# Four scheduling edits in one linear-attention and gated-MLP kernel: Newton steps for pairs of token tiles, weight statistics a step later, sums after divisions, and another product order at the start

## The chip, the cores and the metric

The kernel runs on one core of one Trainium2 chip. The metric is device time in microseconds (us) of that core, from the first to the last instruction, over several executions; medians are given with their range. Executions in which the chip grants the tensor engine a lower clock are kept apart as slow runs; everything compared here counts as fast (mean granted clock 0.999 or 1.000 in the profiled runs, down to 0.996 in some of the others; what this does to the ratios is said below the table of the experiments).

The engines are named as the profile names them: PE is the tensor engine, DVE is VectorE, ACT is ScalarE, POOL is GpSimd, SP is SyncE.

## The reference

```python
# x: 1 x 2048 x 1024 bf16; wqkv: 1024 x 3072; wo: 1024 x 1024; w_gate, w_up: 1024 x 3584; w_down: 3584 x 1024
def _A_ref(x, wqkv, wo):                       # linear attention, 32 heads of 32
    q, k, v = ...                              # split of x @ wqkv
    phi = lambda t: jnp.where(t > 0, t + 1, jnp.exp(t)) + 1e-6
    pq, pk = phi(q), phi(k)
    kv = jnp.einsum("bhsd,bhse->bhde", pk, v)
    z = jnp.einsum("bhsd->bhd", pk)
    num = jnp.einsum("bhqd,bhde->bhqe", pq, kv)
    den = jnp.einsum("bhqd,bhd->bhq", pq, z)[..., None] + 1e-6
    return (num / den)... @ wo

def _B_ref(x, w_gate, w_up, w_down):
    return (silu(x @ w_gate) * (x @ w_up)) @ w_down

xn = _layernorm(A_x)                           # over the 1024 columns of a token
return A_x + _A_ref(xn, ...) * silu(_B_ref(xn, ...))
```

## The kernel before

The 2048 tokens are 16 tiles of 128. The stages, in order of time in the profile of before, are:

- the **K stage** (to 130 us): for each token tile, LayerNorm, four K/V column products of eight matmuls, and the small products `kvz` (phi(K) transposed times V) of the tile before;
- the **Q stage** and its mixes (130 to 218 us): Q products, numerator and denominator products (**ND**), their division, the output product (**S**);
- the last ND and S work, in which S is computed for two tiles at a time with fewer multiplications (**S units**: sums of inputs on DVE, then products called x, w, y and so on) (218 to 250 us);
- gate/up and down, twice (250 to 759 us).

Beside the K and Q stages the gate/up/down weights of the later stages are prepared: loaded, squared and summed for a power-of-two scale, scaled, and turned into differences on POOL.

The LayerNorm of one token tile starts with statistics on DVE, takes 1/sqrt(variance) by Newton steps on POOL, and ends with the normalise on DVE:

```python
def grp_of(i):
    return i                       # one token tile per group
def grp_tiles(gid):
    return [gid]

NR_ITERS = 3
def emit_rstd(gid, eng=None):
    eng = eng or nc.gpsimd
    mv, rstd, tiles = grp_state[gid]
    n = len(tiles)
    # ... a first guess ("seed") with three small DVE operations; y and a are 128 x n
    for _ in range(NR_ITERS):
        eng.tensor_tensor(out=w[:, 0:n], in0=y, in1=y, op=ALU.mult)
        eng.tensor_tensor(out=w[:, 0:n], in0=w[:, 0:n], in1=a[:, 0:n], op=ALU.mult)
        eng.tensor_scalar(out=w[:, 0:n], in0=w[:, 0:n], scalar1=-0.5, scalar2=1.5, ...)
        eng.tensor_tensor(out=y, in0=y, in1=w[:, 0:n], op=ALU.mult)

def ln_pre(i, eng=None):
    emit_stats(i)                  # DVE bn_stats, bn_aggr
    emit_rstd(grp_of(i), eng)
```

The K loop. `emit_N` is the normalise of a tile, `emit_Bev` of columns 0 and 1 is phi (exp and relu on ACT, two operations on DVE for each column):

```python
PRE_AT = {2: (5, 6), 3: (7, 8), 4: (9, 10), 5: (11, 12), 6: (13, 14), 7: (15,)}
for i in range(2, NT):
    for c in range(NCH):                       # 4 columns
        ...
        emit_Bmm(i, c)                         # 8 matmuls
        if c == 0:
            ...
            emit_C(i - 1)                      # kvz, reads phi(K) of tile i-1
        emit_Bev(i, c)
        if c == 3 and i in (4, 5, 6, 7):
            prep(1)                            # one weight a step further
        if i >= 8 and c % 2 == 1:
            k = 2 * (i - 8) + c // 2
            prep(13 * (k + 1) // 16 - 13 * k // 16)
        if c % 2 == 1:
            for k in (PRE_AT[i - 1] if i - 1 in PRE_AT else ...)[c // 2:c // 2 + 1]:
                emit_N(k)                      # normalise a tile whose statistics came one tile earlier
            for k in PRE_AT.get(i, ())[c // 2:c // 2 + 1]:
                ln_pre(k)                      # statistics and Newton of a later tile
```

A step of weight preparation, and the start of the S units:

```python
def prep_step(between=None):
    # ... load a new weight, store a finished one
    k3 = prep_st.popleft()
    if prep_st[1] is not None:
        emit_st0(*prep_st[1])                  # ACT square of a weight loaded two steps ago
    if k3 is not None:
        emit_st1(k3[0], stat_ps[0]())          # PE sum over partitions
    # ...

u["sums"]()                                    # four DVE sums
nds[0]()                                       # ND product of a tile, DVE divisions
u["x"]()
u["w"]()                                       # w needs the first sum
emit_S(1, 3, 0, fx[4])
nds[1]()                                       # needs the PSUM buffer that the divisions read
units[1]["sums"]()
u["y"]()
u["x2"]()
emit_S(1, 3, 1, fx[4])
```

## Time and profile before

| | before |
|---|---|
| median of 3 runs | 764.59 us (764.06 to 765.7) |
| span of the profiled run, granted clock | 763.0 us, 1.000 |
| PE waits listed | 8.51 us in nine waits |
| after the last matmul | about 4.1 us |

The first part of the page gives busy time, share of the span and instruction count of each engine:

```profile
...
PE 750.1 (98%) x3731; PEld 349.4 (46%) x3731; DVE 561.8 (74%) x1058; ACT 376.2 (49%) x526; POOL 290.0 (38%) x400
...
```

PE is busy 98% of the span, so only about 13 us could be had without taking away matmuls. The list of waits of PE says where they are. Each line is the waiting tile and its line in the kernel, what ended the wait, then total us, number of waits, the longest:

```profile
PE nd L713 <- DVE wq_sb L725: 2.6, 1, 2.6
PE warm_ps L560 <- DVE warm L557: 1.5, 1, 1.5
PE kv_ps L525 <- DMA wkv_sb<-in_A_wqkv_dram: 1.5, 1, 1.5
PE q_ps L182 <- DVE pqT L162: 1.2, 2, 0.9
PE kv_ps L525 <- DVE pk_sb L162: 1.1, 2, 0.9
PE kv_ps L525 <- ACT xnT L514: 0.4, 1, 0.4
PE kv_ps L525 <- ACT r_t L160: 0.3, 1, 0.3
```

The largest wait is `nd`, once, for `wq_sb`, which is the division of the ND product before. The timeline of PE has it at 224.64 us (columns: start us, duration us, engine, line, operation, output and inputs, shapes, count; in brackets the idle time just before and its releaser):

```profile
...
224.64 0.64 PE L713 MATMUL nd<-KVZ,pqT 128*128 128x132 bf16 x8 [2.58 <-DVE wq_sb L725]
...
```

The timeline of DVE at the same place shows what the divisions queued behind:

```profile
...
218.19 0.45 DVE L779 TENSOR_TENSOR wq_sb<-oT 128x512 f16<-128x512 bf16 x1
...
221.27 1.26 DVE L782 TENSOR_TENSOR oT<-oT,wq_sb 128x512 f16<-128x512 bf16 x1
...
223.23 1.35 DVE L725 TENSOR_TENSOR wq_sb<-nd,rden 128x384 bf16<-128x384 f32 x3
...
```

The four sums (L779 to L782, the first and the last shown) fill 218.2 to 222.5 us, and the divisions (L725) start at 223.23 us. VectorE takes its instructions in the order of the program (the Trainium skill, "Perfetto Trace Analysis", Tensor Engine Instruction, calls its queue strict FIFO, and no instruction in these lines passes another).

### The profile page before, as it was taken

What the parts mean: (1) busy time and instruction counts of PE and PEld (TensorE: products, weight loads), DVE (VectorE), ACT (ScalarE), POOL (GpSimd) and SP (SyncE); (2) the same over time, 40 slices, a digit from 0 to 9 for tenths busy, and PEclk for the clock granted to TensorE, in tenths of its full rate; (3) what the DMA queues carried; (4) which work ended last, traced back from release to release, by engine and by line L of the source; (5) the groups of instructions that cost most, each with busy time, mean ns of one, the idle gap of its engine ahead of it and who ended that gap; (6) DMA issues with size and microseconds to landing.
All of it is one profiled execution on the core that took longest, in us unless ns stands there. A gap on an engine that the chain in (4) does not pass through costs nothing.

```text
span 763.0 us, 10573 instructions
## 1 busy us (share of the span) xinstructions
PE 750.1 (98%) x3731; PEld 349.4 (46%) x3731; DVE 561.8 (74%) x1058; ACT 376.2 (49%) x526; POOL 290.0 (38%) x400
## 2 busy tenths in 40 slices
PE   8999999999989999999999999999999999999997
PEld 3444444454444444444444444444444444444444
DVE  6788797687587788888889885358676767787335
ACT  4778866799855656666557411132323222211022
POOL 0477899998540265868686000110000000200000
PEclk9999999999999999999999999999999999999999
DMA  9877899859659669897889227398655445530824
GB/s 318 291 153 144 232 297 305 303 121 304 181 169 272 232 228 307 298 348 288 303 296 371 106 82 264 112 342 324 245 185 184 166 165 169 173 141 15 275 89 133
DMA packets 105845, 170.30 MB, mean 223 GB/s; under 512 B 34688, under 2 KB 82176, under 8 KB 95168
## 3 DMA queue, kind: packets, MB, share of 16 engines
q1 hardware_dynamic: 100144, 144.99, 59.2%
q0 software_dynamic: 4208, 22.15, 7.3%
q10 hardware_dynamic: 1440, 2.49, 1.1%
q8 instruction: 29, 0.48, 0.3%
q14 instruction: 24, 0.20, 0.1%
HBM read 111.67 MB, written 50.59 MB: 213 GB/s over the span
## 4 chain that ended last, share of the span: by engine, by line
PE 70%; DVE 1%; ACT 0%; issue 0%
PE zw L935 25%; PE xb L935 13%; PE dzw L1120 12%; PE yb L935 6%; PE dx L1120 6%; PE dy L1120 3%; PE fx L786 3%; PE df L1120 1%; PE dz L1120 0%; PE fx L744 0%; PE nd L713 0%; DVE wq_sb L725 0%; DVE wq_sb L781 0%; DVE oT L782 0%; DVE wq_sb L780 0%; DVE pqT L150 0%
## 5 line engine op out<-in xcount | busy, mean ns | idle before, releaser
L935 PEld LDWEIGHTS <-w_sb 128*128 128x128 f16 (+1 forms) x1568 | 152.1, 98 | 182.8
L525 PE MATMUL kv_ps<-wkv_sb,xnT 128*128 128x512 bf16 x512 | 114.1, 379 | 3.3 <-DMA wkv_sb<-in_A_wqkv_dram 1.5
L935 PE MATMUL xb<-xnT,w_sb 128*128 128x512 bf16 x448 | 115.0, 379 | 0.0
L935 PE MATMUL zw<-S,w_sb 128*128 128x512 f16 x448 | 105.8, 379 | 0.0
L935 PE MATMUL zw<-xnT,w_sb 128*128 128x512 bf16 x448 | 105.8, 379 | 0.0
L294 POOL TENSOR_TENSOR w_sb<-w_sb 128x512 f16<-128x512 bf16 x42 | 50.3, 1197 | 97.8 <-DVE w_sb L282 53.2
L259 ACT ACTIVATE w_sb<-w_sb 128x2048 bf16<-128x2048 bf16 x42 | 79.9, 1903 | 13.1 <-DMA w_sb<-in_B_w_up_dram 6.5
L1120 PE MATMUL dx<-w_sb,hT 128*128 128x512 bf16 x210 | 79.6, 379 | 0.0
L525 PEld LDWEIGHTS <-xnT 128*128 128x128 bf16 x512 | 48.4, 97 | 59.2 <-issue 3.9
L1120 PEld LDWEIGHTS <-hT 128*128 128x128 bf16 (+1 forms) x462 | 45.2, 98 | 51.7
L182 PE MATMUL q_ps<-xnT,wq_sb 128*128 128x512 bf16 x256 | 58.7, 379 | 1.2 <-DVE pqT L162 1.2
L1120 PE MATMUL dzw<-w_sb,hT 128*128 128x512 f16 x196 | 58.3, 379 | 0.0
L1011 ACT ACTIVATE sg<-cg 128x1024 bf16<-128x1024 f32 x28 | 29.6, 1057 | 57.4 <-DVE cg L1004 57.4
L935 PE MATMUL yb<-S,w_sb 128*128 128x512 f16 x224 | 57.4, 378 | 0.0
L1004 DVE SCALAR_TENSOR_TENSOR cg<-zw,rc_all,s 128x1024 f32<-128x1024 f32 x28 | 35.9, 1283 | 25.2 <-PE zw L935 13.5
L1060 POOL TENSOR_TENSOR hs<-hT 128x512 f16<-128x512 bf16 x2 | 2.5, 1255 | 132.6 <-ACT sg L1011 132.6
L963 DVE SCALAR_TENSOR_TENSOR s<-yb,rc_all,s 128x512 f32<-128x512 f32 x42 | 31.4, 748 | 28.0 <-ACT s L962 28.0
L295 POOL TENSOR_TENSOR w_sb<-w_sb 128x512 f16<-128x512 bf16 x42 | 50.8, 1209 | 3.3
L297 POOL TENSOR_TENSOR w_sb<-w_sb 128x512 f16<-128x512 bf16 x42 | 50.5, 1203 | 0.0
L296 POOL TENSOR_TENSOR w_sb<-w_sb 128x512 f16<-128x512 bf16 x42 | 50.1, 1192 | 0.0
L1094 POOL DMA_DIRECT2D out_dram<-io x16 | 8.7, 542 | 101.9 <-DVE io L1093 101.6
L962 ACT ACTIVATE s<-xb,rcl 128x512 f32<-128x512 f32 x14 | 9.6, 687 | 65.3 <-PE xb L935 65.3
(183 smaller groups left out, 1203.2 us busy)
## 6 DMA issues: line engine op xcount, KB each, us to landing
w_sb<-pk_g SPq DMA_DIRECT2D x27, 1024.0 KB, 6.0
pk_g<-w_sb SPq DMA_DIRECT2D x14, 1024.0 KB, 5.0
w_sb<-wd SPq DMA_DIRECT2D x14, 1024.0 KB, 5.3
w_sb<-pk_u SPq DMA_DIRECT2D x14, 1024.0 KB, 5.0
pk_u<-w_sb POOLq DMA_DIRECT2D x13, 1024.0 KB, 5.2
w_sb<-wd SPq DMA_DIRECT2D x14, 768.0 KB, 5.8
w_sb<-in_B_w_gate_dram SPq DMA_DIRECT2D x14, 512.0 KB, 5.9
w_sb<-in_B_w_down_dram SPq DMA_DIRECT2D x28, 256.0 KB, 4.9
```

The lines of the kernel that those rows point to most:

```text
L182: nc.tensor.matmul(q_ps[:], lhsT=wq_sb[:, dc, g * P:(g + 1) * P], rhs=xn_ap(dc, btok), start=(dc == 0), stop=(dc == DC - 1))
L259: nc.scalar.activation(out=junk, in_=raw_view(key, t), func=ACT.Square, accum_out=asum[:])
L294: nc.gpsimd.tensor_tensor(out=T1, in0=b12, in1=b11, op=ALU.subtract)
L295: nc.gpsimd.tensor_tensor(out=T2, in0=b22, in1=T1, op=ALU.subtract)
L296: nc.gpsimd.tensor_tensor(out=T3, in0=b22, in1=b12, op=ALU.subtract)
L297: nc.gpsimd.tensor_tensor(out=T4, in0=b21, in1=T2, op=ALU.subtract)
L525: mm = nc.tensor.matmul(kv_ps[:], lhsT=xn_ap(dc, tok), rhs=wkv_sb[:, dc, c * CW:(c + 1) * CW], start=(dc == 0), stop=(dc == DC - 1))
L935: mm = nc.tensor.matmul(out, lhsT=lhs(k), rhs=rhs(k), start=(first and k == 0), stop=(k == HK - 1), skip_group_check=True)
L963: nc.vector.scalar_tensor_tensor(out=s2[:], in0=y_[:], scalar=rc, in1=s1[:], op0=ALU.mult, op1=ALU.add)
L1004: nc.vector.scalar_tensor_tensor(out=d12, in0=zw[:], scalar=rc, in1=s2[:, None, :].to_broadcast([P, 2, TB]), op0=ALU.mult, op1=ALU.add)
L1011: nc.scalar.activation(out=sg[:, 1:3, :], in_=cf[:], func=ACT.Silu)
L1120: nc.tensor.matmul(out, lhsT=lhs, rhs=rhs, start=first, stop=lastk, skip_group_check=True)
```

## The change

The change has four parts. (1) The Newton steps of two neighbouring token tiles are done in one chain on 128x2 operands, with half as many POOL instructions. (2) The square of a prepared weight comes one step later, so that its load has had longer to land, and the preparations are spread differently: one more before tile 8, 11 in place of 13 in tiles 8 to 15, two in place of one in Q block 0. (3) The sums of the first S unit are issued behind the divisions. (4) At the start of the K stage the second product is that of tile 1, column 0, in place of tile 0, column 1, whose weights come later.

```diff
@@ weights                                                       (part 2)
+    PREP_AT = ((4, 3), (5, 3), (6, 1), (6, 3), (7, 3))
@@ prep_step
-        if prep_st[1] is not None:
-            emit_st0(*prep_st[1])
+        if prep_st[0] is not None:
+            emit_st0(*prep_st[0])
@@ LayerNorm groups                                              (part 1)
+        GRP = {5: (5, 6), 6: (5, 6), 7: (7, 8), 8: (7, 8), 9: (9, 10), 10: (9, 10), 11: (11, 12), 12: (11, 12),
+               13: (13, 14), 14: (13, 14)}
         def grp_of(i):
-            return i
+            return grp_tiles(i)[0]
         def grp_tiles(gid):
-            return [gid]
+            return GRP.get(gid, (gid,))
@@ ln_pre
             emit_stats(i)
-            emit_rstd(grp_of(i), eng)
+            if i == grp_tiles(i)[-1]:
+                emit_rstd(grp_of(i), eng)
@@ start of the K stage                                          (part 4)
         emit_Bev(0, 0)
+        emit_Bmm(1, 0)
+        emit_N(2)
         emit_Bmm(0, 1)
-        emit_N(2)
-        emit_Bmm(1, 0)
+        emit_Bev(1, 0)
+        ln_pre(3)
         emit_Bev(0, 1)
-        ln_pre(3)
-        emit_Bev(1, 0)
@@ K loop and Q block 0                                          (part 2)
-                if c == 3 and i in (4, 5, 6, 7):
+                if (i, c) in PREP_AT:
                     prep(1)
-                    prep(13 * (k + 1) // 16 - 13 * k // 16)
+                    prep(11 * (k + 1) // 16 - 11 * k // 16)
-            if g == 3:
+            if g in (2, 5):
                 prep(1)
@@ S units                                                       (part 3)
-        u["sums"]()
         nds[0]()
         u["x"]()
-        u["w"]()
+        u["sums"]()
         emit_S(1, 3, 0, fx[4])
         nds[1]()
+        u["w"]()
+        emit_S(1, 3, 1, fx[4])
         units[1]["sums"]()
         u["y"]()
         u["x2"]()
-        emit_S(1, 3, 1, fx[4])
```

## The prediction

> **What bounds it now.** TensorE: the page gives 750.1 us busy of 763.0 at full clock. Of the other 12.9 us, 8.6 are nine waits (1.5 at the start) and about 4.1 follow the last matmul. No PE wait lies after 225 us (gate/up/down). List of waits and PE timeline:
> - 2.58 us at 224.6: the second ND product waits for VectorE's divisions of the first (one PSUM buffer), which sit behind the four S-unit sums (218.2 to 222.5).
> - 1.46 us at 11.1: K product (tile 0, column 1) waits for its weight DMA; 0.33 us at 20.7: a bank waits for a ScalarE eviction.
> - 0.18 and 0.95 us late in the K stage, 0.24 and 0.93 us in Q block 0: banks wait for VectorE phi, and that for ScalarE exp.
>
> **What the change does.**
> 1. *Sums behind divisions.* They (0.36 + 0.35 + 1.35 us) can then run from 218.6 to 220.8, while PE has x and an S product until 221.0. Sums took 0.45, 1.20, 1.37, 1.26 us here, 0.42 later; GpSimd ran until 222.2. That agrees with the Trainium skill, "SBUF — State Buffer", Who interferes with whom: two-input VectorE operations contend with GpSimd reads. w and y should find their sums ready. Gain 2.3 to 2.6 us.
> 2. *Newton pairs.* 13 groups become 8; 60 GpSimd operations of 0.26 us go, and 15 VectorE ones of 0.15 us. None is on PE's chain, but GpSimd's Newton ends at 78.5 us and delays the weight differences, which run without gap from 85.7 to 151.8, about 5 us per tile, while 13 preparations were asked for in 59 us (4.5 us each). Stores and loads queue behind.
> 3. *Statistics one step later, preparations respread* (one earlier; 11, not 13, in tiles 8 to 15; two in Q). Before, ScalarE's squares wait 6.6 us in five waits for weight DMAs (list of waits); ScalarE is strict FIFO (Trainium skill, "Perfetto Trace Analysis", Tensor Engine Instruction), so exp and phi come late. At 11 per 59 us GpSimd keeps pace and loads land a step ahead. Of 2.3 us I expect 1.7 to 2.3 back. In the ND stage squares end 1.7 us before their sum matmuls: no new wait. VectorE in Q block 0 gets fuller (estimate 15.8 us of work against 14.3 of PE); five banks cover that.
> 4. *K order.* Product (tile 1, column 0) fills the DMA wait, but needs ScalarE's transposed copy (10.24 us); VectorE's Newton for tile 2 and phi stay bound by the x DMA at 11.74 us, so the tile 2 transpose and the bank freed at 20.6 us come hardly earlier. The wait moves there; net 0.1 to 0.3 us.
>
> **Sum.** 2.5 + 2.0 + 0.15 = 4.6 us. Predicted **760.0 us**, 80% range **758.4 to 762.8**. Faster by over 2%: 0.01; within 2%: 0.98; slower by over 2%: 0.01.
>
> **What would show it.** Right: PE waits after 100 us fall from 4.9 us to under 0.8; no square waits for a DMA in the K stage; GpSimd starts weight differences near 75 us and has gaps before 150; the ND wait is gone; the first 21 us keep 3 to 3.8 us of PE idle, differently named. Wrong on 4: K tile 2 starts a microsecond earlier.
>
> **What would make it wrong.** New PE waits on a square or on phi in Q block 0; w or y waiting for sums; Newton pairs delaying a transpose; a DMA wait as gate/up begins.

## More of the kernel before

The timeline of DVE in the K stage, cut to the last seed operation of a Newton chain (L469) and to the normalise (L482), shows a tile being normalised and another being seeded alternately:

```profile
...
57.55 0.15 DVE L469 TENSOR_SCALAR rstd<-rstd 128x1 int32<-128x1 int32 x1
58.25 0.55 DVE L482 TENSOR_SCALAR xn<-xp,mv,rstd 128x1024 bf16<-128x1024 bf16 x1 [0.55 <-POOL rstd L477]
...
60.65 0.15 DVE L469 TENSOR_SCALAR rstd<-rstd 128x1 int32<-128x1 int32 x1
...
62.92 0.53 DVE L482 TENSOR_SCALAR xn<-xp,mv,rstd 128x1024 bf16<-128x1024 bf16 x1
...
65.30 0.15 DVE L469 TENSOR_SCALAR rstd<-rstd 128x1 int32<-128x1 int32 x1
66.01 0.55 DVE L482 TENSOR_SCALAR xn<-xp,mv,rstd 128x1024 bf16<-128x1024 bf16 x1 [0.55 <-POOL rstd L477]
...
```

The two short waits for POOL are 0.55 us. The normalise at 58.25 us and the one at 66.01 us are 7.76 us apart, for two token tiles' statistics; PE takes 7.37 us for a tile of the K loop. POOL is busy without a gap here: it has two chains of twelve Newton operations to serve per K tile (the work of the K stage for one token tile). No PE wait lies here, so the small lag was covered.

## The result, and the profile after

| | before | after |
|---|---|---|
| median | 764.33 us (763.88 to 765.7, 4 runs) | 765.62 us (765.03 to 766.42, 4 runs) |
| span of the profiled run, granted clock | 763.0 us, 1.000 | 764.6 us, 0.999 |
| PE waits listed | 8.51 us | 9.21 us |

The ratio of the two is 1.0015, with a 95% interval of 0.9997 to 1.0032. Ratios here and below are worked out from the fast runs of the same rounds, so they are not quite the ratio of the medians. The expected 4.6 us did not show. The first part of the page of after:

```profile
...
PE 751.0 (98%) x3731; PEld 349.3 (46%) x3731; DVE 556.3 (73%) x1043; ACT 376.2 (49%) x526; POOL 277.9 (36%) x340
...
```

POOL has the 60 instructions and 12 us less that the change was to take away. The list of waits of PE of after (lines are four or five higher in this kernel than in before):

```profile
PE kvz L551 <- DVE pk_sb L163: 2.8, 4, 1.3
PE kv_ps L529 <- DVE pk_sb L163: 1.5, 1, 1.5
PE warm_ps L565 <- DVE warm L562: 1.5, 1, 1.5
PE xb L940 <- ACT sg L1015: 1.2, 1, 1.2
PE kvz L551 <- ACT w_sb L260: 0.5, 1, 0.5
PE fx L791 <- DVE wq_sb L784: 0.5, 1, 0.5
PE kv_ps L529 <- ACT xnT L518: 0.5, 1, 0.5
PE kv_ps L529 <- DVE xnT L516: 0.3, 1, 0.3
PE tr_ps L513 <- DVE xn L486: 0.2, 1, 0.2
PE yb L264 <- DVE s L968: 0.2, 1, 0.2
```

The large `nd` wait, the two `q_ps` waits and the DMA wait `kv_ps <- wkv_sb` are gone, as intended. In their place stand `kvz` for `pk_sb`, four times, `kvz` once for `w_sb`, and `kv_ps` for `pk_sb`, 1.53 us: together 4.9 us, all in the K stage, where before had no PE wait between 21 and 112 us. `pk_sb` is phi(K). The timeline of PE of after has them at these times (three of the six):

```profile
...
63.80 0.40 PE L551 MATMUL kvz<-v_sb,pk_sb 128*128 128x129 bf16 x4 [0.55 <-DVE pk_sb L163]
...
74.42 0.40 PE L551 MATMUL kvz<-v_sb,pk_sb 128*128 128x129 bf16 x4 [1.29 <-DVE pk_sb L163]
...
87.94 3.61 PE L529 MATMUL kv_ps<-wkv_sb,xnT 128*128 128x512 bf16 x16 [1.53 <-DVE pk_sb L163]
...
```

They come about 9 us apart in pairs. The timeline of DVE of after shows the loop behind them:

```profile
...
53.53 0.17 DVE L473 TENSOR_SCALAR rstd<-rstd 128x2 int32<-128x2 int32 x1
...
54.13 0.69 DVE L163 SCALAR_TENSOR_TENSOR pk_sb<-e_t,r_t 128x512 bf16<-128x512 f32 x1
...
55.19 0.69 DVE L163 SCALAR_TENSOR_TENSOR pk_sb<-e_t,r_t 128x512 bf16<-128x512 f32 x1
58.18 0.55 DVE L486 TENSOR_SCALAR xn<-xp,mv,rstd 128x1024 bf16<-128x1024 bf16 x1 [2.29 <-POOL rstd L481]
...
60.08 0.49 DVE L486 TENSOR_SCALAR xn<-xp,mv,rstd 128x1024 bf16<-128x1024 bf16 x1
...
62.45 0.17 DVE L473 TENSOR_SCALAR rstd<-rstd 128x2 int32<-128x2 int32 x1
...
```

L473 is the last seed operation; L163 is the second half of phi; L486 is the normalise. DVE seeds a pair at 53.53 us, does two phi (to 55.9 us), then stands for 2.29 us until POOL's chain is done, normalises both tiles and takes the statistics of the next pair, and seeds that at 62.45 us: a period of 8.92 us. The timeline of POOL of after, cut to the first, the second and the last of the twelve operations of that pair's chain:

```profile
...
53.78 0.30 POOL L477 TENSOR_TENSOR lnw<-rstd 128x2 f32<-128x2 f32 x1 [4.56 <-DVE rstd L473]
54.15 0.72 POOL L478 TENSOR_TENSOR lnw<-lnw,lna 128x2 f32<-128x2 f32 x1
...
57.95 0.19 POOL L481 TENSOR_TENSOR rstd<-rstd,lnw 128x2 f32<-128x2 f32 x1
```

The chain runs from 53.78 to 58.14 us, 4.4 us; between chains POOL stands idle for 4.56 us. So the period is a sum of two things that no longer overlap: 4.4 us of POOL from seed to last Newton operation, and 4.5 us of DVE from that to the next seed. A K tile of PE is 7.37 us, so DVE falls behind by 1.5 us a tile, and phi with it. Before, the first tile of each pair had a chain of its own that began half a K tile earlier.

To compare parts of the kernels that a single time can't tell apart, the next table gives milestones read from the timeline of PE of each profiled run: the first `kvz` product of the K loop, the first Q product, the first ND product of the last block, the first gate product, the first product of the down stage of the first pass, and the end of the last matmul. All are us from the start of the span.

| run | first kvz | first Q | last block's ND | gate/up 1 | down 1 | last matmul |
|---|---|---|---|---|---|---|
| before | 25.85 | 130.43 | 217.98 | 250.52 | 420.24 | 758.86 |
| after | 25.05 | 134.30 | 220.04 | 250.50 | 421.92 | 760.54 |

After arrives at the first Q product 3.9 us later than before, makes 1.8 us of it good in Q and the mixes and 2.1 us in the last ND block (30.46 us in place of 32.54), and is level at gate/up. Then it loses 1.7 us in gate/up of pass 1 (171.4 us in place of 169.7), where its list of waits has `xb` for `sg`, 1.2 us. The releaser `sg` is an ACT operation, late because a square before it had waited for a weight's DMA, as the timeline of ACT of after shows:

```profile
...
329.75 1.91 ACT L260 ACTIVATE w_sb<-w_sb 128x2048 bf16<-128x2048 bf16 x1 [5.93 <-DMA w_sb<-in_B_w_up_dram]
...
```

### The profile page after: what moved, and what is told of

It is laid out like the page before. It is cut to its first block, busy times and chain, and to the rows that moved or that the text cites. A ratio compares the mean times of both kernels' runs of the same rounds, so it can differ in the third digit from the quotient of the medians.

```text
span 764.6 us, 10494 instructions
## 1 busy us (share of the span) xinstructions
PE 751.0 (98%) x3731; PEld 349.3 (46%) x3731; DVE 556.3 (73%) x1043; ACT 376.2 (49%) x526; POOL 277.9 (36%) x340
## 4 chain that ended last, share of the span: by engine, by line
PE 84%; DVE 6%; POOL 4%; DMA 3%; issue 2%; ACT 1%; SPq 0%; ACTq 0%; POOLq 0%
PE zw L940 23%; PE dzw L1125 12%; PE xb L940 12%; PE q_ps L183 7%; PE dx L1125 6%; PE yb L940 6%; PE kv_ps L529 6%; PE s_ps L749 3%; PE dy L1125 3%; PE fx L791 3%; DVE stats L448 2%; DMA w_sb<-in_B_w_up_dram 2%; POOL lnw L478 1%; DMA xp<-in_A_x_dram 1%; POOL rstd L481 1%
```

## The experiments

Kernels are compared only within the same rounds. The theory that the runs had to test (here theory P, for pairs) is the loop above: the paired chain is long and DVE stands waiting for it, so phi is late. The rival (theory R) is that the later statistics and the respread preparations made the K-stage waits, because they too move DVE and ACT work into tiles 6 to 9.

| run | median us (range, runs) | before | ratio, 95% interval |
|---|---|---|---|
| e0_after_again | 765.16 (764.91 to 766.53, 6) | 765.79 | 0.9999, 0.9983 to 1.0015 |
| e1_no_pairs | 759.82 (759.0 to 762.14, 6) | 765.79 | 0.993, 0.9912 to 0.9948 |
| e2_pairs_only | 771.24 (770.44 to 773.42, 6) | 765.79 | 1.0078, 1.0059 to 1.0097 |
| e3_stats_first | 759.29 (758.69 to 760.36, 6) | 765.79 | 0.992, 0.9904 to 0.9935 |
| e4_two_iters | 758.85 (758.32 to 759.69, 4) | 765.45 | 0.9919, 0.9902 to 0.9935 |
| e5_nd_only | 762.44 (761.96 to 765.8, 4) | 765.45 | 0.9974, 0.9948 to 1.0 |
| e6_korder_only | 765.29 (764.01 to 767.25, 4) | 765.45 | 1.0004, 0.9982 to 1.0026 |
| e7_stats_prep_only | 762.15 (761.86 to 762.81, 4) | 765.45 | 0.9964, 0.9945 to 0.9982 |
| e10_stats_first_again | 759.39 (758.73 to 760.43, 6) | 766.19 | 0.9914, 0.9891 to 0.9938 |
| e8_z_bank | 758.92 (758.6 to 760.79, 6) | 766.19 | 0.9914, 0.9888 to 0.994 |
| e9_z_bank_io | 760.79 (759.0 to 762.66, 6) | 766.19 | 0.9933, 0.9906 to 0.9959 |

All gave the reference's result. All executions counted as fast, but a part of these ratios goes with the granted clock. In the call of e10 the executions of before took 763.82 to 764.5 us at a mean clock of 0.999 or 1.000 (four of them) and 765.68 to 768.26 us at 0.997 or 0.998 (seven), while all executions of e1, e3, e4 and e7 to e10 had 0.999 or 1.000. With the executions at 0.999 or above alone, the plain means give 1.001 for e0, 0.994 for e1, 0.993 for e3, 0.992 for e4, 0.996 for e5, e7 and e9, 1.000 for e6, and 0.994 for e10 and e8 (no interval was worked out for these; e2 has a single such execution). Whether the kernel has a part in the clock is open. The milestones come from profiles at 0.999 or 1.000 and are free of this. The milestones of the profiled runs:

| run | first kvz | first Q | last block's ND | gate/up 1 | down 1 | last matmul |
|---|---|---|---|---|---|---|
| e0_after_again | 25.47 | 134.70 | 220.45 | 250.89 | 420.63 | 759.25 |
| e1_no_pairs | 25.08 | 128.91 | 214.66 | 245.11 | 416.69 | 755.32 |
| e2_pairs_only | 25.32 | 135.12 | 222.79 | 255.33 | 426.77 | 765.39 |
| e3_stats_first | 24.84 | 127.89 | 214.06 | 244.50 | 415.86 | 754.49 |
| e4_two_iters | 24.85 | 127.91 | 214.07 | 244.52 | 414.23 | 752.85 |
| e5_nd_only | 25.48 | 130.02 | 217.55 | 247.99 | 417.71 | 756.33 |
| e6_korder_only | 25.01 | 129.79 | 217.23 | 249.77 | 419.49 | 758.11 |
| e7_stats_prep_only | 25.57 | 129.15 | 214.90 | 247.44 | 417.34 | 755.96 |
| e10_stats_first_again | 25.95 | 129.00 | 215.18 | 245.62 | 415.36 | 753.99 |
| e8_z_bank | 24.91 | 127.97 | 214.16 | 244.36 | 414.09 | 752.71 |
| e9_z_bank_io | 26.52 | 129.58 | 215.75 | 245.94 | 417.42 | 756.04 |

The first column scatters by up to 1.7 us between runs that are the same up to there (24.84 to 26.52 among e3, e4, e8, e9 and e10; 24.84 and 25.95 for one kernel), probably with the landing of the first DMAs, so differences of a few tenths in the other columns mean little until this is taken off.

### After, again

No edit: the changed kernel once more, to see which of its waits belong to it.

> The changed kernel again, unedited, to see which of its waits repeat. Both theories: 765.6 us, and in the trace the same K-stage waits between 60 and 90 us, 4.9 us in sum. Open: the 1.15 us wait of an up product near 335 us on ScalarE, behind a square whose weight DMA took 12.6 us to land (9.7 in the kernel before). If it comes with the change it is there again; if DMA landing varies from run to run, it is gone in some profiles, and times near 765.0 are runs without it, near 766.3 with it.

The K-stage waits came back in kind and size (`kvz` for `pk_sb` 2.8 us in four, `kv_ps` for `pk_sb` 1.5 us), and the first Q product is at 134.70 us. The wait near 335 us did not: gate/up of pass 1 took 169.7 us, as in before. So the K-stage loss belongs to the change, and the gate/up wait of the first profile of after is something that comes and goes. The times fit what was expected of it: four executions lie at 764.91 to 765.18 us (one of them profiled, without the wait) and two at 766.25 and 766.53 (the profiled one of after, with the wait, took 766.42). The executions of before in this call at a clock of 0.999 or 1.000 also fall into two groups, 763.92 to 764.15 and 765.33 to 765.79 us, though no profile of before shows the wait. In time, the kernel was level with before.

### No pairs

```diff
-        GRP = {5: (5, 6), 6: (5, 6), ..., 13: (13, 14), 14: (13, 14)}
+        GRP = {}
```

> The changed kernel with Newton steps per tile again, everything else of the change kept. Theory P (pairs: VectorE's first normalisation of a pair waits for the whole Newton chain that VectorE itself seeded just before, so the chain's 4.4 us enters VectorE's loop, 8.9 us per K tile against 7.37 us of PE): the waits between 60 and 90 us fall from 4.9 to under 1.5, VectorE's waits for GpSimd in the K stage from 15.0 to about 7.5 us, and the time to 760.5 us (759.5 to 762). Theory R (rival: the waits come of the statistics a step nearer their use and the respread preparations, by squares on ScalarE and sums on PE): the waits stay, 765 to 766 us.

The K-stage waits are gone but for one of 0.41 us at 82.56 us, and gate/up starts 5.4 us earlier than in after (245.11 us). DVE waits for POOL 6.8 us in eight waits, in place of 15.0 us in eight. The three other parts without the pairs are worth the ratio 0.993. Theory R, which leaves the K-stage waits in place here, does not hold.

### Pairs only

```diff
 # before, with only part 1
-            return i
+            return grp_tiles(i)[0]
 ...
+            if i == grp_tiles(i)[-1]:
+                emit_rstd(grp_of(i), eng)
```

> The kernel before with Newton pairs and nothing else of the change. Theory P: VectorE's waits for GpSimd near 15 us, PE waits of 3 to 4.5 us between 60 and 90 us; some of the 2.3 us late in K and in Q comes back because GpSimd is freer; time 765.5 to 768.5 us, slower than before. Theory R: no new wait, 762.5 to 764.6 us.

In the list of waits of PE of this run the four `kvz` waits are there with the same 2.8 us:

```profile
PE kvz L550 <- DVE pk_sb L162: 2.8, 4, 1.3
```

The kernel is slower than before by the ratio 1.0078. That is more than was expected: the late K-stage and Q waits of before did not fall away, as I had thought they would with a lighter POOL, but came on top and in the K stage grew (`kv_ps` for `pk_sb` 0.52 us at 116.9 and 1.49 us at 133.4, in place of 0.18 and 0.95; `q_ps` 1.1 us), and this profile has the gate/up wait as well (171.4 us for pass 1). At the start of gate/up the pairs alone cost 4.8 us against before. Between 60 and 90 us the waits sum to 3.5 us here and to 4.9 us in after; part 2 alone has 0.39 us there (below), so about 1 us of the 4.9 comes only when pairs and part 2 are both in.

### Statistics ahead of the normalise

```diff
                 if c % 2 == 1:
+                    for k in PRE_AT.get(i, ())[c // 2:c // 2 + 1]:
+                        ln_pre(k)
                     for k in (PRE_AT[i - 1] if i - 1 in PRE_AT else ...)[c // 2:c // 2 + 1]:
                         emit_N(k)
-                    for k in PRE_AT.get(i, ())[c // 2:c // 2 + 1]:
-                        ln_pre(k)
```

This is after with its pairs, the same operations on the same engines, and only two pieces of DVE work swapped: the seed of a pair now goes ahead of the second normalise of the pair before it, and the next pair's first statistics go ahead of the normalise that waits. So one normalise and one tile's statistics more (0.46 and 1.55 us in this run's trace) lie between a seed and the normalise that needs it.

> The changed kernel with two statements swapped in the K loop: the next tile's statistics and Newton seed are issued before the normalisation of the earlier pair, so Newton runs beside 1.5 to 2 us more of VectorE work. Same instructions in number. Theory P: VectorE's loop falls from 8.9 to about 7 us per tile, its waits for GpSimd from 15.0 to under 5 us, the PE waits between 60 and 90 us nearly go, time 759.5 us (758 to 761.5). Theory R: 765 to 766 us with the waits.

No wait is left between 10 us and the end of the K stage (the `warm_ps` and the two `kv_ps` waits lie before). The whole list of waits of PE of this run:

```profile
PE warm_ps L565 <- DVE warm L562: 1.5, 1, 1.5
PE xb L940 <- ACT sg L1015: 1.2, 1, 1.2
PE fx L791 <- DVE wq_sb L784: 0.5, 1, 0.5
PE kv_ps L529 <- ACT xnT L518: 0.5, 1, 0.5
PE kv_ps L529 <- DVE xnT L516: 0.3, 1, 0.3
```

The timeline of DVE of this run, cut to two first normalises and the last seed operation between them:

```profile
...
54.02 0.55 DVE L486 TENSOR_SCALAR xn<-xp,mv,rstd 128x1024 bf16<-128x1024 bf16 x1
...
56.45 0.17 DVE L473 TENSOR_SCALAR rstd<-rstd 128x2 int32<-128x2 int32 x1
...
61.39 0.55 DVE L486 TENSOR_SCALAR xn<-xp,mv,rstd 128x1024 bf16<-128x1024 bf16 x1
...
```

The chain of this seed runs on POOL from 56.70 to 61.36 us, 4.7 us, so it is no shorter than in after. But DVE does not wait for it, and the first normalises come 7.37 us apart, which is PE's own period. DVE's waits for POOL in the whole run fell to 2.6 us in two. The time is 0.992 of before, and gate/up starts at 244.50 us, 6.0 us earlier than in after. This is the most direct proof: grouping is not slow as such, the order put a latency on VectorE's path. With no pairs (0.993) it is one of two versions of this call that beat both kernels, if by less than 2%, and the times do not tell the two apart (758.69 to 760.36 and 759.0 to 762.14 us). So the swap makes the pairs harmless; that swapped pairs are better than no pairs is not shown, and the swap was not tried without pairs.

### Two Newton iterations

```diff
-        NR_ITERS = 3
+        NR_ITERS = 2
```

> The changed kernel with two Newton steps in place of three (pairs kept, four fewer operations in each chain on GpSimd; still within tolerance by estimate, since the second step leaves a relative error near 5e-6). Theory P: the chain falls from 4.4 to about 3.3 us, so VectorE's loop falls from 8.9 to about 7.8 us per K tile; its waits for GpSimd from 15.0 to 6 to 8 us; PE waits between 60 and 90 us from 4.9 to under 1.2; time 760.5 us (759.5 to 762.5). Against P: no change of the waits, 765 us.

The result was still correct to the test, but what a step less does to its error was not measured, so this is an experiment and not a proposal. The timeline of DVE of this run, cut to two first normalises:

```profile
...
53.94 0.55 DVE L486 TENSOR_SCALAR xn<-xp,mv,rstd 128x1024 bf16<-128x1024 bf16 x1 [1.19 <-POOL rstd L481]
...
61.77 0.55 DVE L486 TENSOR_SCALAR xn<-xp,mv,rstd 128x1024 bf16<-128x1024 bf16 x1 [1.19 <-POOL rstd L481]
...
```

DVE's wait in the loop fell from 2.29 to 1.19 us, the 1.1 us of four POOL operations (0.275 us from start to start of one in the trace of after), and the normalise instructions behind it, 8.91 us apart in after, came 7.83 us apart (53.94 and 61.77 us). No K-stage PE wait was left after 21 us, although the period is still 0.46 us above PE's 7.37: a lag of that size, like the 0.39 us of before, did not reach PE. DVE's waits for POOL in the whole run (5.5 us) and the time (758.85 us) came out below the ranges expected.

### One part at a time

Each of these is before with one part of the change. First the sums behind the divisions (part 3):

```diff
-        u["sums"]()
         nds[0]()
         u["x"]()
-        u["w"]()
+        u["sums"]()
         emit_S(1, 3, 0, fx[4])
         nds[1]()
+        u["w"]()
```

> The kernel before with the S-unit order alone. The stretch from the first ND product of block 3 to the first gate product falls from 32.5 to 30.5 us (in the changed kernel 30.46), with the ND wait of 2.58 us gone and a 0.5 us wait of y for its sums in its place; time 2.0 us below the kernel before of the same rounds (1 to 3).

The last ND block took 30.44 us in place of 32.54, and a wait of 0.47 us of the w product for the first sum stands where 2.58 us stood. In after the timeline of DVE shows why it is left:

```profile
...
221.51 1.35 DVE L730 TENSOR_TENSOR wq_sb<-nd,rden 128x384 bf16<-128x384 f32 x3
222.78 1.38 DVE L784 TENSOR_TENSOR wq_sb<-oT 128x512 f16<-128x512 bf16 x1
224.20 0.43 DVE L785 TENSOR_TENSOR wq_sb<-wq_sb,oT 128x512 f16<-128x512 f16 x1
...
```

The sum at 222.78 us took 1.38 us, the next 0.43 us: POOL was still at its weight differences when the first began. This agrees with what the Trainium skill, "SBUF — State Buffer", Who interferes with whom, says of two-input VectorE operations beside GpSimd reads. I had counted on it and then left it out for this sum. It is not so each time: in before the first sum, at 218.19 us, took 0.45 us although POOL was at its differences too, so when the two collide is not settled here.

Next the product order (part 4):

```diff
+        emit_Bmm(1, 0)
+        emit_N(2)
         emit_Bmm(0, 1)
-        emit_N(2)
-        emit_Bmm(1, 0)
+        emit_Bev(1, 0)
+        ln_pre(3)
         emit_Bev(0, 1)
```

> The kernel before with the order of the first K products alone. As predicted blind: worth 0.1 to 0.3 us. What the traces of the changed kernel and of the one without pairs suggest instead: the first K-V accumulation (25.85 us before) starts 0.4 to 0.9 us earlier, and since the kernel without pairs showed no wait between 21 and 80 us the gain is kept to the end of the K stage; time 0.5 to 1.0 us below before.

The timing can't tell it from before (interval 0.9982 to 1.0026). The expected 0.5 to 1.0 us did not show in time. In the profile the gate/up stage starts 0.75 us earlier than in before, all of which is there at the first `kvz` (0.84 us). The scatter of the first column is larger than that. The four profiles with the old order have the first `kvz` at 25.32 to 25.85 us (median 25.5), the nine with the new one at 24.84 to 26.52 us (median 25.05), so the most that can be said is that this part costs nothing that shows and may gain about half a microsecond.

Last the statistics and the preparations (part 2):

```diff
-        if prep_st[1] is not None:
-            emit_st0(*prep_st[1])
+        if prep_st[0] is not None:
+            emit_st0(*prep_st[0])
 ...
-                if c == 3 and i in (4, 5, 6, 7):
+                if (i, c) in PREP_AT:
 ...
-                    prep(13 * (k + 1) // 16 - 13 * k // 16)
+                    prep(11 * (k + 1) // 16 - 11 * k // 16)
 ...
-            if g == 3:
+            if g in (2, 5):
```

> The kernel before with the statistics one step later and the respread preparations alone, Newton per tile. If the blind prediction's point 3 holds: the four waits late in K and in Q block 0 (2.3 us, and about 0.16 us more for each, as a stopped PE also loses the overlap of its last matmul) go, the first gate product starts 2 to 3 us earlier than 250.5, time 2.5 us below before (1.5 to 3.5). If instead the preparations need the freer GpSimd of the pairs, the waits stay and less than 1 us is gained.

All four late waits (0.18, 0.95, 0.24 and 0.93 us in before) are gone, no square waits for a DMA in the K stage, and one new wait of 0.39 us appears at 82.79 us. Gate/up starts 3.1 us earlier than in before. No run separates the later square from the respread preparations.

Now the parts can be added, at the start of gate/up and against before. For parts 2 and 3 the difference that is already there at the first `kvz` (0.28 and 0.37 us) is taken off as scatter, since these parts change nothing up to there; for part 4 it is the effect itself, and is left in. Part 3 then gives −2.2 us (2.1 of it in the last ND block), part 2 −2.8 us and part 4 −0.75 us, together −5.7 us. The run without pairs, which has all three, measured −5.4. The pairs give 5.4 us back, and after stands at 0.0.

### Two further steps on the best version

The first run is a repeat of the swapped kernel, as a base on the same chip.

> The same kernel as the run with the statistics of a tile ahead of its normalise, again, as the base of the next two on one chip. The theory that the paired Newton chain made a loop of 8.9 us on VectorE expects no PE wait for phi between 50 and 100 us and 0.991 to 0.994 of the time of before (about 759.3). If the wait of 1.15 us near 335 us (second gate/up steps, ScalarE square behind a weight DMA) comes and goes with the landing of that DMA, it may be absent here although the kernel is the same.

It had 0.9914 of the time of before, no K-stage wait after 21 us, and this time no wait near 335 us: gate/up of pass 1 took 169.7 us, where the earlier profile of the same kernel had 171.4 us. The changed kernel and its repeat had shown the same: one kernel can do both.

The next moves the last plain S product ahead of the w product, into a PSUM bank that is idle there:

```diff
         nds[1]()
+        emit_S(1, 3, 1, fx[2])
         u["w"]()
-        emit_S(1, 3, 1, fx[4])
```

> The run above, and in the first S unit the last plain S product moved ahead of the w product and into the idle bank Z. If the 0.49 us wait of w is only the first sum ending late, the product (about 1.7 us of PE work) covers it: the wait is gone, and the stretch from the first ND product of block 3 to the first gate product shortens by 0.5 to 0.7 us (30.44 to about 29.9). Rival: the sums wait for the divisions and the product only moves the wait to y or to x2; then the stretch stays at 30.4. Time against the run above: 0.3 to 0.7 us less, which 5 rounds may just not resolve.

The wait (0.47 us in the base, 0.49 in after) is gone, and the third ND product of the block comes 7.84 us after the first, in place of 8.49. But the stretch to the first gate product shortened by only 0.24 us (30.20 in place of 30.44): the fourth ND product starts 1.08 us after the product before it, in place of 0.86, and the product after it 0.75 us later, in place of 0.56, gaps too small for the list of waits. So the expectation held at the place itself, but 0.4 us of the 0.65 was lost again, as the rival said, if at the fourth ND product and not at y or x2. Why PE starts later there is open. In time it is the same as the base (758.92 and 759.39 us, both 0.9914): not resolved.

The last one moves five loads of x and s, which are needed only at the end of the pass, away from 300 to 320 us, since they are issued among the weight loads for which ACT waited:

```diff
-                if first and i in range(6, 11):
+                if first and i in range(14, 19):
                     io_load(mb)
```

> The run above, and the five loads of x and s for the later output moved from gate/up steps 6 to 10 to steps 14 to 18, away from the weight loads that land near 325 us. If those loads crowd the weight DMA (12.6 us to land in one run, 9.7 in another), ScalarE's squares near 324 us wait less than 2 us and no PE wait is near 335 us; gate/up pass 1 takes 169.7 us. If they have nothing to do with it, the wait may appear as before (pass 1 of 171.4 us), and a single profile can't say more than that it did or did not.

There was no wait near 335 us, but gate/up of pass 1 took 171.5 us all the same. Two of its PE waits, 0.5 and 0.9 us, now lie at 377 and 380 us. The timeline of ACT of this run, before them:

```profile
...
372.09 1.91 ACT L260 ACTIVATE w_sb<-w_sb 128x2048 bf16<-128x2048 bf16 x1 [4.31 <-DMA w_sb<-in_B_w_up_dram]
...
```

The loads now are issued at 365.4 to 368.6 us, with a weight's load among them at 366.70 us, and a square waited 4.31 us for that load. The wait moved to where the loads went, but not because the load was slow: it landed after 5.28 us, as in the run before (5.41 us). It was issued 120.8 us after the start of gate/up in place of 117.8, 1.3 us of that behind two of the moved loads on the same queue. The wait near 335 us is of another kind: its load was issued at 317.05 us in after and at 316.90 us in the repeat, and landed after 12.6 us in the one and 9.2 us in the other. What decides when that weight lands late is left open, and this run does not show that the x and s loads do. The move itself is no gain (0.9933).

## Why the prediction was wrong, and where it was right

The points are numbered as in the prediction: its point 1 is part 3 of the change, point 2 is part 1, point 3 is part 2, and point 4 is part 4.

**The step that failed is in point 2, "None is on PE's chain".** The prediction counted the Newton operations by their busy time and found them away from PE, so the pairs cost nothing and freed POOL. They cost 5.4 us at the start of gate/up (after against the run without pairs), 4.8 us alone. What the runs show in its place:

- The chain of twelve POOL operations is a latency, and pairing does not shorten it. On 128x2 an operation takes 0.19 us as it does on 128x1, and they follow each other every 0.275 us. Fewer chains are a gain in throughput only.
- The first tile of a pair now waits for the statistics of the second. The seed falls half a K tile later, with only two phi between it and the normalise that needs it. DVE, in the order of the program, stands still for 2.29 us and holds back the phi behind it.
- DVE and POOL then take turns, 4.4 and 4.5 us, and the loop of 8.92 us exceeds the 7.37 us of PE. Swapping two DVE blocks, or shortening the chain, removed all K-stage waits after 21 us. Theory P is shown by taking the loop apart in three different ways (no pairs, order, chain length), and R is refuted, since its part alone gained time and made one wait of 0.39 us.

The prediction could have had this. The trace of before has POOL's start-to-start time, 0.275 us, so a chain is at least 3.3 us (an estimate from that number), and in fact shows chains of 3.4 to 4.5 us on POOL. It also has the phi of a column at about 1.1 us on DVE, so two of them cover 2.2 us. The instruction order of the changed kernel shows nothing else between seed and normalise. The prediction named "Newton pairs delaying a transpose" as a risk, but its range ends at 762.8 us; and what was delayed is phi, not a transpose.

The Trainium skill, "Perfetto Trace Analysis", Optimizing Scalar/DVE Operations, has both sides of this. It says "Grouping and performing larger operations can improve throughput if the engine is saturated", and also that where ScalarE and VectorE are not saturated but cause bubbles on other engines, breaking up instructions may let work finish sooner. The section is about those two engines, and the grouped operations here are POOL's. In the sense of the first sentence, POOL had no gap from 35 to 78 us in before, and its busy time fell by 12 us. In the sense of the second, PE waited 2.8 and 1.5 us for phi from VectorE, 73% busy, and without pairs 0.41 us of these waits was left.

**"Newton's end delays the weight differences"; "GpSimd starts weight differences near 75 us".** In after the first difference starts at 83.56 us, later than in before (80.43 us): the seeds of the Newton chains come late from DVE's loop, and the chains stand in front of the differences on POOL. With the swap the first difference starts at 75.64 us, so the gain was there to be had.

**Point 1, sums behind divisions.** The mechanism was right. The size was 2.1 us, not 2.5, because "w and y should find their sums ready" was wrong by 0.49 us for w.

**Point 3, statistics and preparations.** Right, and too small: 2.8 us, where 2.0 was in the sum. In after no square waits for a DMA before 300 us, as predicted. The listed waits fell by 1.9 us (2.3 gone, 0.39 new). A stop of PE also costs more than its listed wait: a 512-column matmul is recorded with 379 ns while they follow each other every 216 ns. The recorded end is a model and not a measurement, as the Trainium skill, "Perfetto Trace Analysis", Tensor Engine Instruction, says, and this trace agrees; so about 0.16 us are missing from a wait that follows such a matmul. Three stops fewer are an estimated 0.5 us. The rest, 0.4 us, I can't name.

**Point 4, product order.** The direction was right. The DMA wait of 1.46 us went and smaller ones came (0.23 us for `xn`, 0.3 us for `xnT` in after). Its size, 0.5 to 0.8 us in the profiles against 0.15 expected, is not settled against the scatter. The first 21 us were to keep 3 to 3.8 us of PE idle; the waits listed there are 3.6 us in before and 2.5 us in after.

**"PE waits after 100 us fall from 4.9 us to under 0.8".** Not so as it stands: in after they are 1.84 us. It is right up to 250 us (0.49 us). The 1.35 us in gate/up in that profile belong to waits that before, the repeat of after and six more of the eleven runs do not have, so they can't be put down to the change. Why a weight lands late in some executions is open.

**Sum.** Expected −4.6 us. Measured at the start of gate/up: −2.2 −2.8 −0.75 +5.4 = −0.35 us by the separate profiles, 0.0 by that of after. In whole times, after is 1.0015 of before and its repeat 0.9999, so the change is worth nothing that can be resolved.

## What to carry to other kernels

When small dependent operations are grouped to save instructions, write down for each group when its input is complete and who needs its output next: the latency of a chain does not shrink when two chains become one, and the first member of a group waits for the last. Where two in-order engines hand work to each other, add up the loop (here 4.4 + 4.5 us) and compare it with the time per step of the bottleneck (7.37 us), even when neither engine is full. If the loop is too long, try to issue the producer of the next round ahead of the consumer of this one before giving up the grouping: here that swap turned a change of nothing into 0.8 to 0.9% less time by the ratios, 0.6 to 0.7% among executions at a clock of 0.999 or above. Giving up the grouping did about as well (0.7 and 0.6%), so measure both.

## What the Trainium skill lacked or had wrong

- "GPSIMD Engine Reference", Elementwise — side-by-side cycle accounting: it has times for long operations, and names the dispatch of a POOL instruction without a duration (its section on instruction dispatch has "tens of cycles" for one part of it). Here a dependent chain of 128x1 or 128x2 operations on POOL advances one operation every 0.275 us, with 0.19 us recorded for each.
- "SBUF — State Buffer", Who interferes with whom: it has the rule but no figure for what it does to a chain of tiny operations. Four of the twelve Newton operations that ran while DVE did phi took 0.24 to 0.72 us in place of 0.19, so the chain took 4.4 us where twelve undisturbed steps would be 3.3.
- "Perfetto Trace Analysis", Optimizing Scalar/DVE Operations: it names grouping as a gain in throughput for a saturated engine. Beyond the sentence on breaking up instructions, it doesn't say that grouping postpones the first member's result: 5.4 us were lost here by that, and got back by an order of issue.
- No page gives the scatter of load times: in one profile of the swapped kernel an ACT square near 324 us waited 5.88 us for a 512 KB weight load that took 12.6 us to land, and in the repeat of the same kernel it took 9.1 us and there is no wait there.
